# Gated mix of linear attention and squared-relu layer: hidden tiles fetched four and split two steps ahead, attention a step farther behind its numerators, the query-weight fold three products sooner

## The chip, the cores and the metric

The kernel runs on one core of one Trainium2 chip. The metric is the device time of one launch in microseconds, the median of several runs. The engines are TensorE (PE in the profile), VectorE (DVE), ScalarE (ACT), GpSimd (POOL) and SyncE (SP), whose queue issues nearly all DMA transfers here.

## The reference, cut to what matters

The output mixes two branches of the same input x (2048 rows, 512 columns) with one gate per row. Branch A is linear attention with 32 heads of 16 columns and a softmax feature map. Branch B is a dense layer with 1792 hidden units, whose activation is the square of relu.

```python
qkv = split_heads(x @ wqkv)                       # 32 heads of 16
pq = einsum("bhsd,hdf->bhsf", q, w_phi)           # the same for k
phi = concat([softmax(p), softmax(-p)])           # 32 features per head
kv, z = phi_k^T V, sum(phi_k)
o = (phi_q kv) / (phi_q z + 1e-6)
a = o @ wo
b = relu(x @ w1 + b1)**2 @ w2 + b2
g = sigmoid((x * gate_w).sum(-1))
return g * a + (1 - g) * b
```

## The kernel before, in words

**Products.** Everything is fp32. A product is made of three fp32r matmuls (`mm3`, L59 to 63): both factors are split into a high part (a copy on ACT, L56) and a low part (a subtraction on DVE or POOL, L57), and high·high (L61), high·low (L62) and low·high (L63) are added in one bank. L61 and L62 need only the first factor's high part; L63 needs its low part. Names ending in h and l are these parts.

**First stages, up to about 272 us of the span.** The product x·w1 is computed by a seven-product scheme (banks uX, uY, uZ) and merged with the keys and values (banks kX, kY, kZ). Relu and square give the hidden activations. They don't stay on the chip: each 128x512 tile is written to DRAM (`hkept`). Near the end comes `fold("q")` (L254): 128 small matmuls fold the feature map's weights `wphi` into the query weights, in four banks; four DVE transposes (L268) bring them to SBUF, and `wq_ready` splits them. The list `seq` holds the order of these products on PE, and `at(n, f)` hangs a call on a place in it.

**Last stage, the loop over t = 0 to 55.** A step t is one hidden tile: `down(t, c)` adds its product with a 128-row piece of w2 to four banks, in 12 matmuls of 128x512. I call these twelve d0, d1 and so on. Each tile is fetched from DRAM by `h_fetch` (tile `hin`), and `h_ready` splits it: `hh` on ACT, `hl` on POOL. There are four buffers for each of hh and hl (tags O0 and O1, two buffers each), and four for the ring "in", which hin shares with xnin, xin and wphi.

Branch A of one pair of 128-row pieces is a group p = 0 to 7, and `starts[p]` is its first step. The table `steps` says which of its parts come before which d:
- `do_q` of each of two pieces: 12 matmuls (I number these 16 projections q0 to q15), then on DVE the largest and smallest value of each head (L305, L306) and two subtractions (L307, L308), the exponential on ACT (L310), and sums and reciprocals on DVE (L315, L317).
- `do_q_scaled`: two products with z on POOL (`ez`, L508), a reduction and small operations on DVE (L510 to L517), the scaling (L321) and a transpose to `tb` (L525). After the second piece, tb is regrouped into `phiT` by four copies on ACT (L534) and twelve DMAs on SP (L536).
- `do_n`: 32 small matmuls give the numerators (`num`, L544; num0 to num7 by p), split to `oh` on ACT and `ol` on DVE.
- `attend` of each piece: 12 matmuls with the weights wo (att0 to att15), then a sum on DVE (L586) and, when both branches have met, the write of the row.

`gate_load` and `gate_dot` (tile xnin, L407) and `gates` (`ge`, L412) make the gates of the next 512 rows; `x_again` fetches the next x (xA... from `xkept`, or xin from the input, split to xS10 and xS11).

**What sets the order.** PE's order is the order of the code (`manual_schedule` for PE). DVE, ACT, POOL and the DMA queue are ordered by the scheduler, which follows the code's order, its own estimate of readiness, and priorities (`ahead`). On the chip every engine and every queue works in order: an instruction that waits holds up all behind it.

Of the kernel before, what the change touches and what calls it, by code (L numbers as in the profile page):

```python
# [21 lines left out]
NC = SB // P  # L22
# [13 lines left out]
def tile_gated_mix(ctx: ExitStack, tc: tile.TileContext, xT, xn, wqT, wkT, wphi, wv, wo, w1, b1, w2, b2, gw, out):  # L36
# [217 lines left out]
    def fold(nm):  # L254
        wph, t = st["wphi"], st["wT", nm]
        pss = [bank(f"fold{nm}") for r in range(4)]
        for g in range(NK):
            for q in range(4):
                for r in range(4):
                    rows, cols = slice(32 * r, 32 * r + 32), slice(g * P + 32 * r, g * P + 32 * r + 32)  # L260
                    nc.tensor.matmul(pss[r][32 * q:32 * q + 32, g * P:(g + 1) * P], wph[rows, cols],
                                     t[g][rows, :].rearrange("r (k q i) -> r k q i", q=4, i=32)[:, :, q, :],
                                     start=True, stop=True, skip_group_check=True)
        w = work.tile([P, 2, 4, NG, 32], F32, tag="phiT", name=f"w{nm}in", bufs=1).rearrange(
            "p u r g s -> p (u r g s)").rearrange("p (k g r s) -> p k g r s", k=NK, g=NK, r=4)
        for r in range(4):
            with ahead():
                nc.vector.transpose(w[:, :, :, r, :].rearrange("p k g s -> p g k s"),  # L268
                                    pss[r].rearrange("p (g k i) -> p g k i", g=NK, i=32))
        st["w", nm] = [w[:, k].rearrange("p g r s -> p (g r s)") for k in range(NK)]  # L270
# [219 lines left out]
    def h_fetch(t):  # L490
        i, f = divmod(t, NF)
        raw["h", t] = load(ring("hin"), hkept[ORDER_B[i], f])

    def h_ready(t):
        hi, lo = st["h", t] = [work.tile([P, 512], F32R, tag=f"O{t % 2}{j}", name="h" + j, bufs=2) for j in "hl"]
        split(raw["h", t], hi, lo, nc.gpsimd)
# [164 lines left out]
    seq, extra = [], {}  # L661
    at = lambda i, f, *a: extra.setdefault(i, []).append(lambda: f(*a))
# [105 lines left out]
    with tc.manual_schedule(engines={mybir.EngineType.PE}):  # L768
        warm_up()
        opening()  # L770

        us = u_stream([(0, g) for g in range(3, NPF)], (0, 2))
        vs = v_stream([(0, m, "kv") for m in range(NC)])
        seq = merged(us, vs)
        n0 = len(seq)
        PER = 15
        for g in range(3, NPF):
            b = PER * (g - 3)
            if g > 3:
                at(b - 8, w_sums, g, POOLE)  # L780
                at(b - 4, w_ready, g, 1)
            at(b + 1, w_ready, g, 2)
            at(b + 2, w_last, g, POOLE)
            at(b + 6, w_ready, g, 3)
            if g > 3:
                at(b + 1, w_save, g, 0)
            else:
                at(b + 1, w_save, g, 0)
            at(b + 3, w_save, g, 1)
            at(b + 5, w_save, g, 2)  # L790
            at(b + 9, w_save, g, 3)
            if g + 1 < NPF:
                at(b + 2, w_fetch, g + 1)
                at(b + 8, w_ready, g + 1, 0)
        at(24, x_fetch, 1)
        at(30, x_fetch2, 1)
        for kk in range(2):
            at(n0 - 14 + 2 * kk, x_sums, kk, ("S1", "S2"), POOLE)

        n1 = n0  # L800
        us1 = u_stream([(1, g) for g in range(NPF)])
        vs1 = v_stream([(1, m, "kv") for m in range(NC)], (0, NC - 1, "kv"))
        seq1 = merged(us1[:len(us1) - 5], vs1) + us1[len(us1) - 5:]
        seq += seq1
        for i, op in enumerate(XOPS):
            for kk in range(2):
                at(n0 + i - (4 if i < 3 else 1), x_ready, op, kk)
        for kk in range(2):
            at(n0, x_sums, kk, ("S3",), POOLE)
            at(n0 + 2, x_sums, kk, ("S4",), POOLE)  # L810
        per = len(seq1) / NPF

        def o1_raw():
            raw["w", 0, 0] = load(ring("w1in"), w1[0])

        at(n0 - 12, o1_raw)
        at(n0 - 6, w_ready, 0, 0)
        for g in range(NPF):
            b = n0 + int(per * g)
            if g:  # L820
                at(b - 9, w_again, g, 0)
            at(b - 7, w_again, g, 1)
            at(b - 3, w_again, g, 2)
            at(b + 2, w_again, g, 3)
        at(n0 + 4, lambda: nc.sync.dma_start(gwb, gw.partition_broadcast(P)))
        for c in range(NC):
            n = ORDER_B[0] * NC + c
            at(n0 + 10 + 3 * c, gate_load, n)
            at(n0 + 14 + 3 * c, gate_dot, n)
        at(n0 + 24, gates, ORDER_B[0])  # L830
        for i in range(0, NF, 4):
            fs = range(i, min(i + 4, NF))
            at(n0 + 9 + 3 * i, w2_prepare, fs)
            for k, f in enumerate(fs):
                at(n0 + 12 + 3 * i + 2 * k, w2_split, k, f)
        n2 = len(seq)

        def q_fetch():
            t = work.tile([P, 4 * D], F32, tag="tb", name="wqin", bufs=1)
            load_fold("q", wqT, [t[:, k * D:(k + 1) * D] for k in range(NK)])  # L840
            st["wphi"] = load(ring("wphi"), wphi)

        at(n2 - 20, q_fetch)
        seq.insert(n2 - 2, lambda: fold("q"))
        n2 += 1
        for f in range(4):
            at(n2 - 5 + f, w2_again, f)
        at(n2 - 1, h_fetch, 0)
        at(n2 - 1, h_fetch, 1)
        run()  # L850


        steps = {}
        when = lambda s, f, *a: steps.setdefault(s, []).append(lambda: f(*a))
        NT = NB * NF
        starts = (2, 7, 12, 18, 24, 30, 36, 42)
        for k in range(NK):
            when(0, wq_ready, k)
        x_again(0)
        when(1, kv_burst, (1, NC - 1, "kv"))  # L860
        when(3, kv_done)
        when(0, b2_load)
        for k in range(NK):
            when(4 + k, wo_fetch, k)
            when(6 + k, wo_ready, k)
        when(8, x_again, 1)
        when(starts[3] + 3, x_again, 2)
        when(starts[5] + 3, x_again, 3)
        for i in range(1, NB):
            b, s = ORDER_B[i], starts[2 * i] - 8  # L870
            for c in range(NC):
                when(s + c, gate_load, b * NC + c)
                when(s + 2 + c, gate_dot, b * NC + c)
            when(s + 6, gates, b)
        for p, s in enumerate(starts):
            for c in range(2):
                when(s + 2 * c, do_q, p, c)
                when(s + 2 * c + (3 if p == 0 else 1), do_q_scaled, p, c)
            when(s + 10, do_n, p)
            for c in range(2):  # L880
                when(s + 12 + c, attend, p, c)
        h_ready(0)
        for t in range(NT):
            for f in steps.get(t, ()):
                f()
            i, f = divmod(t, NF)
            if t + 2 < NT:
                h_fetch(t + 2)
            if t + 1 < NT:
                h_ready(t + 1)  # L890
            for g in (2 * t + 4, 2 * t + 5):
                if g < NF:
                    w2_again(g)
            if f == 0:
                st["d"] = [ubank(f"d{c}") for c in range(NC)]
            last = t == NT - 1
            now = () if t == NT - 2 else (t - 1, t) if last else (t,)
            for c in range(NC - 1 if last else NC):
                for u in now:
                    down(u, c)  # L900
            if last:
                ends = [bank(f"end{j}") for j in range(2)]
                sc = slice((NC - 1) * P, NC * P)
                for j, s in enumerate(halves):
                    for u in now:
                        mm3(ends[j][:, s], st["h", u], st["w2", u % NF], sc, s, u == now[0], u == t)
            if f < NF - 1:
                continue
            for c in range(NC):
                n = ORDER_B[i] * NC + c  # L910
                evict(n, st["d"][c], ALL)
                if last and c == NC - 1:
                    for e, d, s in zip((nc.sync, nc.scalar), ends, halves):
                        evict(n, d, s)
                        e.dma_start(out[n * P:(n + 1) * P, s], st["f", n][:, s])
                else:
                    out_done(n)
# [47 lines left out]
```

## Time and profile before

| | us |
|---|---|
| median of 3 runs | 558.26 |
| the three runs | 555.23, 558.42, 558.26 |
| the profiled execution's own time | 554.75 |
| its span in the trace | 553.0 |
| the loop's part of the span | from 272.7 (d0) to 549.4 |
| DMA moved | 108.92 MB, mean 197 GB/s |
| ACT busy in the span | 244.3, 44% |
| POOL busy in the span | 236.4, 43% |

The table is of one core, so there is no slower core to look for. A profile row of the timeline reads: start, duration, engine, line, operation, what is written <- what is read, shape, how many instructions in a row; in brackets the idle time just before and what ended it. SPq is the queue that issues DMAs; such a row's duration is the issue, not the transfer. A matmul of the loop has a duration of 0.39 us but overlaps with the next, so what counts is the distance between starts.

### The profile page before, as it was taken

Reading aid. Unit: us, or ns where it says so; the run is one execution under the profiler, and the core shown is the slowest. Engines: PE = TensorE matmul, PEld = TensorE weight load, DVE = VectorE, ACT = ScalarE, POOL = GpSimd, SP = SyncE. Lnnn points to the kernel's source line nnn. Section 1 sums busy time; section 2 is a strip of 40 time slices with the busy share of each in tenths; the row PEclk is TensorE's granted clock in tenths of the full one; section 3 lists DMA queues with packets and bytes.
Section 4 is the critical chain, followed back from the end, with each engine's and each line's share of the span. In section 5 each row is a group of like instructions: output and inputs, shape, how many; then the busy total and the mean of one; then the engine's idle time right before and its main releaser. Section 6 shows DMA issues by size and latency. Waiting matters only on the chain.

```text
span 553.0 us, 9651 instructions
## 1 busy us (share of the span) xinstructions
PE 505.1 (91%) x3532; PEld 396.2 (72%) x3532; DVE 425.7 (77%) x607; ACT 244.3 (44%) x399; POOL 236.4 (43%) x190
## 2 busy tenths in 40 slices
PE   7587679999998999999899699989999969999997
PEld 3355458877776888788688577767787848777776
DVE  4986759979999967766858989997879684787503
ACT  5485546446666565645543234242314323332320
POOL 3945743274235356320525434534345433434320
PEclk9799869999999999999999979989999998999999
DMA  8458487854368998999877363756235523135312
GB/s 299 176 210 307 153 286 261 292 197 162 115 211 293 317 347 295 336 353 335 299 257 239 95 192 104 234 152 200 84 122 156 146 79 95 39 83 166 82 35 76
DMA packets 66167, 108.92 MB, mean 197 GB/s; under 512 B 8264, under 2 KB 18248, under 8 KB 66120
## 3 DMA queue, kind: packets, MB, share of 16 engines
q1 hardware_dynamic: 65800, 107.91, 58.9%
q8 instruction: 28, 0.46, 0.4%
q10 hardware_dynamic: 288, 0.39, 0.2%
q14 instruction: 19, 0.16, 0.1%
q0 software_dynamic: 32, 0.01, 0.0%
HBM read 60.30 MB, written 41.68 MB: 184 GB/s over the span
## 4 chain that ended last, share of the span: by engine, by line
PE 45%; DVE 23%; DMA 11%; issue 7%; ACT 6%; SPq 5%; POOL 4%; DVEq 0%; POOLq 0%; ACTq 0%
PE d L61 5%; PE d L62 5%; PE d L63 5%; PE att L63 3%; SPq L536 2%; DMA w1in<-in_w 2%; DVE e L308 2%; PE att L62 2%; PE att L61 2%; PE uY L63 2%; PE uY L61 2%; DMA hin<-hkept 2%; DVE e L321 2%; PE uY L62 2%; DVE sm L315 2%
## 5 line engine op out<-in xcount | busy, mean ns | idle before, releaser
L57 POOL TENSOR_TENSOR hl<-hin,hh 128x512 fp32r<-128x512 f32 x56 | 73.7, 1325 | 130.9 <-ACT hh L56 128.1
L56 ACT ACTIVATE hh<-hin 128x512 fp32r<-128x512 f32 x56 | 34.7, 627 | 95.3 <-PE d L62 34.4
L221 POOL TENSOR_TENSOR t<-t,t 128x512 f32<-128x512 f32 x28 | 41.5, 1485 | 46.9 <-ACT t L220 34.3
L508 POOL TENSOR_TENSOR ez<-e,z 128x512 f32<-128x512 f32 x32 | 42.6, 1351 | 36.3 <-ACT e L310 31.0
L310 ACT ACTIVATE e<-e 128x1024 f32<-128x1024 f32 x32 | 33.8, 1058 | 47.3 <-DVE e L308 47.0
L315 DVE TENSOR_REDUCE sm<-e 128x64 f32<-128x1024 f32 x32 | 38.9, 1217 | 19.6 <-ACT e L310 19.5
L197 ACT ACTIVATE c<-c,b1c 128x512 f32<-128x512 f32 x42 | 29.9, 718 | 33.0 <-DVE c L212 33.0
L198 ACT ACTIVATE c<-c 128x512 f32<-128x512 f32 x56 | 34.8, 627 | 1.1
L534 ACT ACTIVATE phiT<-tb 32x512 f32<-32x512 f32 x32 | 20.1, 628 | 32.1 <-DVE tb L525 26.9
L480 POOL TENSOR_TENSOR w2in<-w2in,w2h 128x512 fp32r<-128x512 f32 x14 | 20.2, 1464 | 29.8 <-DMA w2in<-in_w 20.0
L510 DVE TENSOR_REDUCE dz<-ez 128x64 f32<-128x1024 f32 x16 | 19.5, 1218 | 17.2 <-POOL ez L508 17.2
L321 DVE TENSOR_TENSOR e<-e,w 128x1024 f32<-128x1024 f32 x16 | 21.6, 1350 | 0.3
L212 DVE TENSOR_TENSOR c<-uY,t 128x512 f32<-128x512 f32 x28 | 18.8, 676 | 3.9 <-PE uY L63 3.9
L321 DVE TENSOR_TENSOR e<-e,r 128x1024 f32<-128x1024 f32 x16 | 21.0, 1314 | 0.2
L525 DVE STREAM_TRANSPOSE tb<-e 128x1024 f32<-128x1024 f32 x16 | 19.7, 1238 | 0.3
L305 DVE TENSOR_REDUCE mx<-q 128x32 f32<-128x512 f32 x16 | 10.8, 675 | 9.0 <-PE q L63 9.0
L317 DVE RECIPROCAL r<-sm 128x64 f32<-128x64 f32 x32 | 17.4, 543 | 0.2
L57 DVE TENSOR_TENSOR ol<-num,oh 128x512 fp32r<-128x512 f32 x16 | 10.2, 677 | 9.1 <-ACT oh L56 9.1
L586 DVE SCALAR_TENSOR_TENSOR row<-b2b,rest,att 128x512 f32<-128x512 f32 x8 | 5.9, 739 | 14.6 <-PE att L63 14.6
L153 POOL TENSOR_TENSOR T23in<-w1in 128x256 f32<-128x256 f32 x6 | 6.1, 1009 | 23.0 <-DMA w1in<-in_w 23.0
L407 DVE SCALAR_TENSOR_TENSOR xnin<-xnin,gwb 128x512 f32<-128x512 f32 x16 | 14.0, 877 | 0.0
L61 PE MATMUL att<-woVt,oh 128*128 128x512 f32 x32 | 13.4, 419 | 0.0
(533 smaller groups left out, 1633.1 us busy)
## 6 DMA issues: line engine op xcount, KB each, us to landing
hkept<-c SPq DMA_DIRECT2D x56, 256.0 KB, 3.5
hin<-hkept SPq DMA_DIRECT2D x56, 256.0 KB, 2.9
phiT<-tb SPq DMA_DIRECT2D x96, 64.0 KB, 2.0
xin<-in_xT SPq DMA_DIRECT2D x20, 256.0 KB, 5.4
xnin<-in_xn SPq DMA_DIRECT2D x16, 256.0 KB, 2.8
out<-row SPq DMA_DIRECT2D x15, 256.0 KB, 2.2
w1in<-in_w SPq DMA_DIRECT2D x14, 256.0 KB, 3.7
w2in<-in_w SPq DMA_DIRECT2D x14, 256.0 KB, 4.2
```

Of the source, the lines that this page charges most:

```text
L56: nc.scalar.activation(hi, src, AF.Copy)
L57: elo.tensor_tensor(lo, src, hi.bitcast(F32), ALU.subtract)
L61: nc.tensor.matmul(o, ah[:, sa], bh[:, sb], start=first, stop=False, **kw)
L62: nc.tensor.matmul(o, ah[:, sa], bl[:, sb], start=False, stop=False, **kw)
L63: nc.tensor.matmul(o, al[:, sa], bh[:, sb], start=False, stop=last, **kw)
L197: nc.scalar.activation(t, src, AF.Relu, bias=b1c[:, f:f + 1])
L198: nc.scalar.activation(t, t, AF.Square)
L221: nc.gpsimd.tensor_tensor(t, t, st["t1", u], ALU.add)
L310: nc.scalar.activation(ef, ef, AF.Exp)
L315: nc.vector.tensor_reduce(sm, e3, AX.X, ALU.add)
L321: eng.tensor_tensor(e3, e3, w.unsqueeze(2).to_broadcast([P, 2 * H, DH]), ALU.mult)
L508: nc.gpsimd.tensor_tensor(ez[:, hs, :], e3[:, hs, :], zbc[half], ALU.mult)
```

## The change

The diff changes the schedule only; the arithmetic stays as it was.

```diff
-        seq.insert(n2 - 2, lambda: fold("q"))
+        seq.insert(n2 - 5, lambda: fold("q"))
...
-        at(n2 - 1, h_fetch, 0)
-        at(n2 - 1, h_fetch, 1)
+        for t in range(4):
+            at(n2 - 4 + t, h_fetch, t)
...
-        starts = (2, 7, 12, 18, 24, 30, 36, 42)
+        starts = (2, 7, 12, 18, 24, 30, 36, 41)
...
-                when(s + 2 + c, gate_dot, b * NC + c)
+                when(s + 1 + c, gate_dot, b * NC + c)
...
-                when(s + 12 + c, attend, p, c)
+                when(s + 13 + c, attend, p, c)
         h_ready(0)
+        h_ready(1)
         for t in range(NT):
...
+            if t + 4 < NT:
+                h_fetch(t + 4)
             if t + 2 < NT:
-                h_fetch(t + 2)
-            if t + 1 < NT:
-                h_ready(t + 1)
+                h_ready(t + 2)
```

In words: the fold stands three products sooner; hidden tiles are fetched four steps ahead instead of two, and split two steps ahead instead of one; each attend stands a step later; each gate dot a step sooner, and the last group starts at step 41 instead of 42.

On PE the attend of a group, put one step later, also changes places with the projections of later groups. In the words used above, the twelve-matmul items after three of the num read:

```
before  num1 d17 q6  d18 att2 d19 att3 q7  d20 d21 num2
after   num1 d17 q6  d18 d19  att2 q7  d20 att3 d21 num2
before  num3 d28 d29 att6 q10 d30 att7 d31 q11 d32 d33 num4 d34 d35 att8 q12 d36
after   num3 d28 d29 q10 d30 att6 d31 att7 q11 d32 d33 num4 d34 d35 q12 d36 att8
```

The other engines' orders come from the scheduler, so the built order is shown at three places.

First, POOL and the DMA queue ahead of num0. POOL's rows of before, where the two ez of a piece are POOL's part of q1, q2 and q3 in the last three pairs:

```order
L57 TENSOR_TENSOR hl<-hin,hh 128x512
L508 TENSOR_TENSOR ez<-e,z_3288 128x512
L508 TENSOR_TENSOR ez<-e,z_3290 128x512
L57 TENSOR_TENSOR hl<-hin,hh 128x512 x2
L508 TENSOR_TENSOR ez<-e,z_3288 128x512
L508 TENSOR_TENSOR ez<-e,z_3290 128x512
L57 TENSOR_TENSOR hl<-hin,hh 128x512 x3
L508 TENSOR_TENSOR ez<-e,z_3288 128x512
```

POOL's rows of the changed kernel, at the same pairs:

```order
L57 TENSOR_TENSOR hl<-hin,hh 128x512 x2
L508 TENSOR_TENSOR ez<-e,z_3296 128x512
L508 TENSOR_TENSOR ez<-e,z_3298 128x512
L57 TENSOR_TENSOR hl<-hin,hh 128x512 x2
L508 TENSOR_TENSOR ez<-e,z_3296 128x512
L508 TENSOR_TENSOR ez<-e,z_3298 128x512
L57 TENSOR_TENSOR hl<-hin,hh 128x512 x2
L508 TENSOR_TENSOR ez<-e,z_3296 128x512
```

Before, the group "x3" behind q2's ez is hl of steps 9, 10 and 11; now steps 9 and 10 stand ahead of q2's ez, and 11 and 12 behind it.

The DMA queue (SP) of before, from the fetches of steps 10 and 11 to the transfers of phiT for num0:

```order
L69 DMA hin<-hkept 128x512
L69 DMA xin<-in_xT 128x512 x2
L69 DMA hin<-hkept 128x512 x2
L428 DMA xA110h<-xkept 128x512
L428 DMA xA110l<-xkept 128x512
L428 DMA xA111h<-xkept 128x512
L536 DMA phiT<-tb 32x2x256 x12
L69 DMA hin<-hkept 128x512 x4
```

The same queue of the changed kernel, from the fetch of step 11:

```order
L69 DMA hin<-hkept 128x512
L69 DMA xin<-in_xT 128x512 x2
L69 DMA hin<-hkept 128x512
L428 DMA xA110h<-xkept 128x512
L536 DMA phiT<-tb 32x2x256 x12
L69 DMA hin<-hkept 128x512 x4
L428 DMA xA110l<-xkept 128x512
L69 DMA hin<-hkept 128x512 x2
```

Ahead of phiT stands now the fetch of step 12 instead of steps 10 and 11, and one xA instead of three. The fetch of step 12 takes a ring buffer that hl of step 11 frees, where that of step 11 took one from hl of step 9.

Second, ACT around the numerators of num1. Before:

```order
L310 ACTIVATE e<-e 128x1024
L56 ACTIVATE hh<-hin 128x512 x2
L412 ACTIVATE ge<-lg 128x4
L56 ACTIVATE oh<-num_3963 128x512
L56 ACTIVATE oh<-num_3964 128x512
L534 ACTIVATE phiT<-tb 32x2x256 x4
```

And in the changed kernel:

```order
L310 ACTIVATE e<-e 128x1024
L56 ACTIVATE hh<-hin 128x512 x2
L56 ACTIVATE oh<-num_3973 128x512
L56 ACTIVATE oh<-num_3974 128x512
L534 ACTIVATE phiT<-tb 32x2x256 x4
L56 ACTIVATE hh<-hin 128x512
L412 ACTIVATE ge<-lg 128x4
```

The gate's exponential (ge) stands now behind both oh and the copies of phiT.

Third, the DMA queue around phiT for num4, where the x of the last 512 rows (xin) is fetched. Before:

```order
L575 DMA out<-row 128x512 x2
L69 DMA hin<-hkept 128x512 x2
L69 DMA xin<-in_xT 128x512 x2
L69 DMA hin<-hkept 128x512
L536 DMA phiT<-tb 32x2x256 x12
L575 DMA out<-row 128x512
```

In the changed kernel:

```order
L69 DMA xnin<-in_xn 128x512
L69 DMA hin<-hkept 128x512 x2
L536 DMA phiT<-tb 32x2x256 x12
L575 DMA out<-row 128x512
L69 DMA xin<-in_xT 128x512 x2
L69 DMA hin<-hkept 128x512
```

The two xin stand now behind phiT's twelve transfers and behind a write of a row, which waits for the sum of att6 on DVE. On DVE their low parts (xS10l, xS11l) have moved from ahead of q10's features to ahead of q11's.

## The prediction

> **What bounds the kernel now.** I read the page first, then PE's waits, then PE's clock by stretches of the loop, and at each stretch that loses time the timelines of the engines around it. The page's busy time:
>
> ```profile
> PE 505.1 (91%) x3532; PEld 396.2 (72%) x3532; DVE 425.7 (77%) x607; ACT 244.3 (44%) x399; POOL 236.4 (43%) x190
> ```
>
> PE is the bound: it misses 48 us of 553.0, much of that in the first stages. What the change can win is what PE loses in the loop. PE's waits, with the total, the number of times and the longest (only the rows on d and att, which belong to the loop):
>
> ```profile
> PE att L63 <- DVE ol L57: 6.1, 5, 4.6
> PE d L63 <- POOL hl L57: 3.7, 1, 3.7
> PE d L61 <- DVE c L212: 2.3, 1, 2.3
> PE att L61 <- ACT oh L56: 1.3, 1, 1.3
> PE d L61 <- ACT hh L56: 0.6, 1, 0.6
> ```
>
> These are 14.0 us of idle time. To them comes what a slower clock costs behind the long ones. The windows view, by stretch:
>
> ```profile
> core 0: us, PE busy (x) PEld busy (x) DVE busy (x) ACT busy (x) POOL busy (x), PEclk, DMA share, GB/s
> 315.00:320.00 5.00, 2.16 (x5) 1.78 (x6) 5.00 (x6) 0.63 (x1) 4.02 (x3) 0.69 0.30 87
> 320.00:325.00 5.00, 5.00 (x15) 3.90 (x15) 3.69 (x6) 2.96 (x5) 1.28 (x1) 0.62 0.78 233
> 365.00:370.00 5.00, 3.42 (x11) 2.37 (x11) 4.97 (x12) 4.31 (x9) 0.00 (x0) 0.81 0.51 147
> 450.00:455.00 5.00, 0.42 (x1) 0.42 (x2) 4.36 (x8) 0.00 (x0) 2.91 (x3) 0.85 0.28 88
> 455.00:460.00 5.00, 5.00 (x13) 3.84 (x13) 3.25 (x4) 2.40 (x4) 0.00 (x0) 0.50 0.16 43
> ```
>
> PE is fully busy in 455 to 460 and yet does 13 matmuls: the granted clock is 0.50. So there are three losses: before 325 (d9), at 366 (att2) and at 450 to 460 (att8). PE's timeline at the first:
>
> ```profile
> 313.43 0.50 PE L61 MATMUL d<-w29h,hh 128*128 128x512 f32 x1 [0.57 <-ACT hh L56]
> ...
> 317.84 0.79 PE L63 MATMUL d<-w29h,hl 128*128 128x512 f32 x1 [3.68 <-POOL hl L57]
> 318.43 0.63 PE L61 MATMUL d<-w29h,hh 128*128 128x512 f32 x1
> ...
> 323.12 0.63 PE L63 MATMUL d<-w210h,hl 128*128 128x512 f32 x1
> ...
> 325.74 0.39 PE L61 MATMUL d<-w211h,hh 128*128 128x512 f32 x1
> ...
> 328.55 1.85 PE L544 MATMUL num<-phiT,kvb 64*32 64x256 f32 x32
> 330.33 0.50 PE L61 MATMUL q<-wq0h,xS10h 128*128 128x512 f32 x1
> ```
>
> From 318.43 to 323.12 lie 11 spaces of 0.426 us; d11, twelve matmuls from 325.74 to 328.55, takes at most 0.234 each. Thirteen slow matmuls cost 13 x 0.19 = 2.5 us. Idle time is 4.25 us, so the place costs 6.7.
>
> **The change part by part.** Hidden tiles sooner. The causes of the wait at d9, from the timelines of POOL, SP and DVE, and the page's row on the landing of phiT and xin:
>
> ```profile
> 313.00 3.56 POOL L508 TENSOR_TENSOR ez<-e,z 128x512 f32<-128x512 f32 x2 [6.97 <-ACT e L310]
> 316.52 2.50 POOL L57 TENSOR_TENSOR hl<-hin,hh 128x512 fp32r<-128x512 f32 x2
> ...
> 313.26 4.88 SPq L69 DMA_DIRECT2D hin<-hkept  x2
> 319.62 8.14 SPq L536 DMA_DIRECT2D phiT<-tb  x12
> ...
> 316.49 1.23 DVE L525 STREAM_TRANSPOSE tb<-e 128x1024 f32<-128x1024 f32 x1
> ...
> phiT<-tb SPq DMA_DIRECT2D x96, 64.0 KB, 2.0
> xin<-in_xT SPq DMA_DIRECT2D x20, 256.0 KB, 5.4
> ```
>
> hl of step 9 stood on POOL behind the ez of q2, which waited until 313.00. In the new order it stands ahead of them, so d9 no longer waits, and PE reaches num0 6.7 us sooner. But num0 needs phiT, and phiT is not sooner by as much. tb is ready at 316.49 + 1.23 = 317.7. SP now meets the fetch of step 12, whose buffer hl of step 11 frees; that hl is the first behind ez on POOL, done at about 316.52 + 1.25 = 317.8. Two issues of 0.4 us later, at 318.7, phiT starts: 0.9 us before 319.62. The end of num0 is set by phiT in both kernels (8.14 us of issues and 2.0 of landing give 329.8, and q4 starts at 330.33). So PE now stands from about 321 to 327.6, and the 6.7 us is not won but moved. Behind a wait that long I expect the slow clock as in the rows above. My value: 2.5 - 0.9 = +1.6 us. Lower end: phiT starts at tb's end and nothing is slowed, -1.9; upper end: slow clock and 1 us of later issue, +3.5. I take +1.6, since the wait is nearest to the 3.68 and 4.61 us that did slow PE.
>
> [...]
>
> The other fetches and splits are at no cost: in the loop's later steps no row of PE's waits names hl or hh. SP issues as many transfers as before. The gate dot one step sooner moves 0.7 us of DVE work within a stretch where DVE does all the waiting work in order anyway: nothing.
>
> Attend a step later, at att2. ACT's and PE's timelines:
>
> ```profile
> 365.63 0.20 ACT L412 ACTIVATE ge<-lg 128x4 f32<-128x4 f32 x1 [4.68 <-DVE xnin L407]
> 365.74 1.07 ACT L56 ACTIVATE oh<-num 128x512 fp32r<-128x512 f32 x2
> ...
> 366.37 0.50 PE L61 MATMUL att<-woXS40h,oh 128*128 128x512 f32 x1 [1.30 <-ACT oh L56]
> ...
> 367.38 0.50 PE L63 MATMUL att<-woXS40h,ol 128*128 128x512 f32 x1 [0.28 <-DVE ol L57]
> ```
>
> oh stood behind ge, which waited for the gate dots on a late DVE. Now oh stands ahead of ge, and att2 comes one d (2.7 us) later. Both alone cover 1.58 us. Gone are 1.58 us of idle and some eight slow matmuls (1.5), with 0.3 for restarting: -3.4. Ends: -3.4 and 0.
>
> At att8, from the timelines of PE, DVE and SP:
>
> ```profile
> 442.77 1.09 PE L544 MATMUL num<-phiT,kvb 64*32 64x256 f32 x32
> 454.58 0.80 PE L63 MATMUL att<-woXS40h,ol 128*128 128x512 f32 x1 [4.61 <-DVE ol L57]
> ...
> 430.30 0.69 DVE L57 TENSOR_TENSOR xS11l<-xin,xS11h 128x512 fp32r<-128x512 f32 x1 [2.06 <-ACT xS11h L56]
> 444.26 0.65 DVE L305 TENSOR_REDUCE mx<-q 128x32 f32<-128x512 f32 x1
> 453.84 1.28 DVE L57 TENSOR_TENSOR ol<-num,oh 128x512 fp32r<-128x512 f32 x2
> ...
> 427.07 7.62 SPq L536 DMA_DIRECT2D phiT<-tb  x12
> ```
>
> ol stands on DVE behind q11's chain: from its features at 444.26 to ol 9.6 us. That chain was late since q10's features waited for xS11l. Now att8 stands behind q12 and d36, so 2 x 2.7 = 5.4 us later than today's 449.97, at 455.4. PE as a whole comes about 2.1 us sooner by the terms above and att4's, so ol is wanted at 453.3. Is it there? xin is now issued behind phiT and a write: 427.07 + 7.62 + 0.5 = 435.2, lands 5.4 later at 440.6, two copies on ACT and two subtractions on DVE end at about 443.2, then q11's chain, 9.6: ol at 452.8. That is 0.5 us of margin if DVE and SP come no sooner than today. They do: q10 is projected one item sooner and doesn't wait for xin, and phiT, with it xin, follows a DVE that has lost 2.06 us of waiting and the lateness from 366; that adds up to 3 us. So the wait goes, 4.61 us of idle and 13 slow matmuls (2.5): -7.2 with 0.1 of restart. Ends: -7.2 and 0.
>
> Three other att waits, what is left of the first row (6.1 - 4.6 - 0.3 = 1.2 us), are 0.4 to 0.5 us each, and 2.7 us more lead covers them: -1.2. Ends: -2.6, with restarts and all, and 0. After them nothing is late next but DVE's own chain; PE goes on with d.
>
> The fold, from DVE's timeline:
>
> ```profile
> 264.06 0.69 DVE L364 TENSOR_TENSOR k<-kY,t 128x512 f32<-128x512 f32 x1 [2.03 <-PE kY L63]
> 272.24 1.22 DVE L321 TENSOR_TENSOR e<-e,r 128x1024 f32<-128x1024 f32 x1
> 273.38 2.50 DVE L268 STREAM_TRANSPOSE wqin<-foldq 128x512 f32<-128x512 f32 x4
> ```
>
> Its four banks include kY's, which L364 frees at 264.75, just where the fold now stands on PE: a wait of some 0.8 us. The four transposes come ahead of L321 and of the uY evictions (L212) on DVE. The 2.3 us that d0 waited for such an eviction goes over to the last product, and the kvps matmuls that need L321's result come no sooner. Best end: the 2.3 goes and 0.8 comes, -1.5. Worst end: kvps comes later by the 2.50 us of transposes, +2.5. I take 0, between them.
>
> Sum: 0 + 1.6 - 3.4 - 7.2 - 1.2 = -10.2 us. Against the profiled execution's 554.75 this is 544.6; that execution is 3.5 us under the median of 558.26, from which it would be 548.1. Runs lie at both places, so I subtract from the middle, 556.5: 546.3 us.
>
> **The rivals.** One: att8 still waits. For it: the margin of 0.5 us, and two more issues ahead of xin, of which the write waits for att6's sum on DVE. Against it: the lead that q10 gains. Price: 7.2 back, 553.5.
>
> Two: the time before num1 governs all. DVE was busy throughout 315 to 320 and 4.97 of 5.00 in 365 to 370; if the slack moves but DVE is still late, att2 and att8 both wait: 546.3 + 10.6 = 556.9, no change. Against it: at 450 to 455 DVE too has idle time, so that lateness is one of order.
>
> Three, slower: phiT late at every num, as at num0. Place: the fetches four steps ahead stand on SP before phiT, wait for hl on POOL, and hl for ez. At num4 today phiT is complete at 427.07 + 7.62 + 2.0 = 436.7, 6.1 us before 442.77. If the queue holds phiT up by 10 us at three of the num, each waits 4 us and loses 2.5 to the clock: 19.5, thus 565.8. It decides from a delay of about 9 us on. For it: num0 shows it; against it: the 6.1.
>
> Four, better: num0 costs nothing or less, and the restarts go too. From 554.75: -1.9 - 3.4 - 7.2 - 2.6 = 539.7.
>
> That the deeper fetch does nothing, as hh and hl have four buffers already, would leave the wait at d9 and take away num0's: 544.7, within the forecast.
>
> **How the numbers follow.** Forecast 0.62 (541 to 550 by itself), rival one 0.14, two 0.08, three 0.06, four 0.10. A measurement of this kernel can tell about 1% from no change, 5.6 us: faster means below 552.7. Faster: 0.62 + 0.10 and 0.06 of rival one, where part of att8's wait is won, 0.78; within 1%: 0.08 of one and 0.08 of two, 0.16; slower: 0.06. The range 539 to 554 leaves out two and three and little more.
>
> **What would show it.** In the changed profile PE's waits should have no d behind hl, and no att behind oh or a long ol; num0 should wait 6 to 7 us for phiT, with a granted clock near 0.5 behind it; att2 and att8 should run into d without a gap. Wrong would be: an att8 still idle for ol (then xin's place is to be looked at), a num other than num0 that waits for phiT, a fold that waits longer than 1 us with kvps late.

## The result, and the profile after

The changed kernel is slower by about 0.9%, which is under the 1% that the prediction called no change: 560.1 us against 555.65 us, medians of 20 runs each, ratio 1.0087 with a 95% interval of 1.0064 to 1.0110. The forecast was 546.3 us and the range 539 to 554. The profiled execution of the changed kernel took 560.03 us.

The page of the changed kernel, its span and busy times:

```profile
span 558.2 us, 9654 instructions
PE 506.3 (91%) x3532; PEld 398.8 (71%) x3532; DVE 423.1 (76%) x607; ACT 244.3 (44%) x399; POOL 239.9 (43%) x190
```

The engines do the same work. Not all of the 5.2 us between the two spans belongs to the change. The timelines of TensorE give the last matmul of the last kY product, up to which TensorE's order is the same, and the last matmul of all; in the changed kernel:

```profile
267.65 0.39 PE L63 MATMUL kY<-KT41h,A221l 128*128 128x512 f32 x1
...
554.48 0.28 PE L63 MATMUL end<-w213h,hl 128*128 128x256 f32 x1
```

and in the kernel before:

```profile
263.63 0.39 PE L63 MATMUL kY<-KT41h,A221l 128*128 128x512 f32 x1
...
549.15 0.28 PE L63 MATMUL end<-w213h,hl 128*128 128x256 f32 x1
```

From there to the end are 285.5 us before and 286.8 after. Second profiles of both (below) gave 284.4 and 289.4, and start times of 266.6 and 265.7. So the first stages vary by 2 to 3 us from run to run, and what follows the last kY, the fold included, lost 1 to 5 us. Nothing of the 10.2 us forecast is left in the time. TensorE's waits in the changed kernel, the rows from the fold on:

```profile
PE d L61 <- DVE row L598: 6.1, 2, 4.2
...
PE uY L61 <- DMA O3h<-wkept: 4.4, 1, 4.4
...
PE num L544 <- DVE ge L415: 3.4, 1, 3.4
...
PE num L544 <- DMA phiT<-tb: 1.9, 1, 1.9
```

No att waits any more, and no d waits for hl: 14.0 us of the old waits are gone. In their place stand 15.8 us in these four rows: a hidden-layer product for its weights O3h, num0 twice, and two d that wait for evictions (L598). An eviction is the DVE operation that reads a finished bank, so that the next products may use it. The profile puts num0's longer wait down to the gates' ge because that ended just then; num0 doesn't read ge. It reads phiT, whose twelve issues run from 326.57 to 334.36 in this kernel, so both of its waits are taken for phiT. The windows view shows the slow clock behind them (columns as in the prediction: the clock is the third number from the right):

```profile
280.00:285.00 5.00, 4.29 (x10) 3.46 (x11) 1.36 (x3) 2.84 (x6) 0.00 (x0) 0.50 0.93 298
335.00:340.00 5.00, 3.94 (x35) 2.41 (x36) 4.93 (x11) 2.44 (x5) 1.76 (x2) 0.50 0.88 261
420.00:425.00 5.00, 3.91 (x12) 3.18 (x13) 4.84 (x7) 2.61 (x5) 3.48 (x3) 0.76 0.43 156
490.00:495.00 5.00, 2.72 (x7) 2.17 (x8) 5.00 (x8) 3.25 (x5) 2.58 (x3) 0.59 0.39 95
```

In three of the four, DVE is busy for 4.84 to 5.00 of 5 us. The stretches between the ends of the num tell where time went, in us from one end to the next:

| stretch | before | after |
|---|---|---|
| last kY to the kvps matmuls | 14.5 | 19.9 |
| to the end of num0 | 52.3 | 50.5 |
| num0 to num1 | 26.3 | 27.0 |
| num1 to num2 (att2) | 29.5 | 25.7 |
| num2 to num3 | 29.1 | 28.5 |
| num3 to num4 (d28) | 28.6 | 32.0 |
| num4 to num5 (att8) | 36.0 | 28.5 |
| num5 to num6 (d42) | 29.2 | 35.5 |

(The table is read off the timelines of the two kernels; behind num6 the items differ.) The first row runs from start to start, the second from the start of the kvps matmuls. The forecast gains at att2 and att8 came, 3.8 and 7.5 us; they were paid back at the fold (5.4), at d28 (3.4) and at d42 (6.3).

The fold, timelines of TensorE and of the DMA queue in the changed kernel:

```profile
275.95 0.39 PE L63 MATMUL uZ<-S41h,O1l 128*128 128x512 f32 x1
280.70 0.76 PE L61 MATMUL uY<-A220h,O3h 128*128 128x512 f32 x1 [4.36 <-DMA O3h<-wkept]
...
273.21 0.99 SPq L69 DMA_DIRECT2D hin<-hkept  x1
274.25 0.42 SPq L488 DMA_DIRECT2D w28l<-w2kept  x1
275.51 0.32 SPq L181 DMA_DIRECT2D O3h<-wkept  x1
```

O3h has one buffer. An earlier uY product frees it, and it is reloaded for the last uY. Before, the fold (1.9 us) and three products stood between the two; now only the products do. The fold, moved ahead of both, covers nothing of the reload, and on the DMA queue the reload stands behind a hidden tile and w2 tiles and goes out at 275.51.

At d42, timelines of DVE and TensorE:

```profile
489.03 0.65 DVE L305 TENSOR_REDUCE mx<-q 128x32 f32<-128x512 f32 x1
...
490.81 0.67 DVE L308 TENSOR_TENSOR e<-mn,q 128x512 f32<-128x512 f32 x1
491.40 1.39 DVE L598 SCALAR_TENSOR_TENSOR row<-d,rest,row 128x512 f32<-128x512 f32 x2
...
492.28 0.77 PE L61 MATMUL d<-w20h,hh 128*128 128x512 f32 x1 [4.23 <-DVE row L598]
```

A block of 14 steps ends with d41; d42 needs its bank empty. Here q14 stands ahead of d41 (start 41 and not 42), so q14's features stand ahead of the eviction on DVE, and nothing stands between d41 and d42 on TensorE. Before, att10 and q14 stood between them.

### The profile page after: what moved, and what is told of

Its sections match the earlier page's. It is cut to its first block, busy times and chain, and to the rows that moved or that the text cites. A ratio compares the mean times of both kernels' runs of the same rounds, so it can differ in the third digit from the quotient of the medians.

```text
span 558.2 us, 9654 instructions
## 1 busy us (share of the span) xinstructions
PE 506.3 (91%) x3532; PEld 398.8 (71%) x3532; DVE 423.1 (76%) x607; ACT 244.3 (44%) x399; POOL 239.9 (43%) x190
## 4 chain that ended last, share of the span: by engine, by line
PE 52%; DVE 22%; DMA 10%; issue 6%; POOL 4%; ACT 3%; SPq 3%; DVEq 0%; POOLq 0%; ACTq 0%
PE d L61 7%; PE d L62 7%; PE d L63 7%; PE att L61 2%; PE att L62 2%; PE att L63 2%; DMA hin<-hkept 2%; DMA w1in<-in_w 2%; DVE e L308 2%; PE uY L63 2%; PE uY L61 2%; PE q L61 2%; PE uY L62 2%; PE q L62 2%; PE q L63 2%
## 5 line engine op out<-in xcount | busy, mean ns | idle before, releaser
L57 POOL TENSOR_TENSOR hl<-hin,hh 128x512 fp32r<-128x512 f32 x56 | 76.4, 1369 | 143.9 <-ACT hh L56 132.8
L221 POOL TENSOR_TENSOR t<-t,t 128x512 f32<-128x512 f32 x28 | 43.7, 1564 | 44.7 <-ACT t L220 32.1
L508 POOL TENSOR_TENSOR ez<-e,z 128x512 f32<-128x512 f32 x32 | 42.0, 1334 | 23.9 <-ACT e L310 23.7
L480 POOL TENSOR_TENSOR w2in<-w2in,w2h 128x512 fp32r<-128x512 f32 x14 | 19.6, 1423 | 32.2 <-DMA w2in<-in_w 20.4
L510 DVE TENSOR_REDUCE dz<-ez 128x64 f32<-128x1024 f32 x16 | 19.4, 1215 | 16.6 <-POOL ez L508 16.6
L525 DVE STREAM_TRANSPOSE tb<-e 128x1024 f32<-128x1024 f32 x16 | 19.9, 1241 | 0.3
L544 PE MATMUL num<-phiT,kvb 64*32 64x256 f32 x256 | 10.2, 411 | 5.4 <-DVE ge L415 3.4
L61 PE MATMUL d<-w20h,hh 128*128 128x512 f32 x16 | 8.4, 525 | 6.1 <-DVE row L598 6.1
```

The lines of the kernel that those rows point to most:

```text
L57: elo.tensor_tensor(lo, src, hi.bitcast(F32), ALU.subtract)
L61: nc.tensor.matmul(o, ah[:, sa], bh[:, sb], start=first, stop=False, **kw)
L221: nc.gpsimd.tensor_tensor(t, t, st["t1", u], ALU.add)
L508: nc.gpsimd.tensor_tensor(ez[:, hs, :], e3[:, hs, :], zbc[half], ALU.mult)
```

## The experiments

All ratios are to the kernel before, run on the same chip. Theory A said that the losses are places, each to be undone by itself. Theory C said that DVE is the bound in the loop, so that a wait taken away comes back where TensorE next needs DVE. The other letters are explained in the expectations.

**The fold back.** Edit of the changed kernel:

```diff
-        seq.insert(n2 - 5, lambda: fold("q"))
+        seq.insert(n2 - 2, lambda: fold("q"))
```

> The changed kernel with the fold back two products before the end. Theory A (the fold used to cover the reload of the w1 tile O3h, whose single buffer the product uY39 frees): the 4.4 us wait of the last uY for O3h and the slow clock behind it go, d0's 2.3 us wait for an eviction comes back, last kY to kvps takes about 14.5 us as before instead of 19.9, and the time falls by about 5 us from the changed kernel's, to a ratio to before of about 0.998. Rival B (the reload is late because four hidden-tile fetches now stand ahead of it in the DMA queue): the wait for O3h stays at 3 us or more, ratio about 1.009 as for the whole change. In both the 4.2 us wait of d42 for the eviction stays.

Measured: 554.38 us, ratio 1.0003 (0.9968 to 1.0038), 0.8% under the whole change. The last uY waits 0.4 us and no longer for O3h; last kY to kvps takes 12.9 us, less than in the kernel before, as d0's wait is gone too. Theory A holds for this place; by rival B of the expectation the wait would have stayed. The edit also changes the order of the DMA queue, so by itself it doesn't part the two causes; the fold alone, below, is for that.

**The start back.** Edit of the changed kernel (with a start of 42 the last attends would fall behind the last step, so they stay):

```diff
-        starts = (2, 7, 12, 18, 24, 30, 36, 41)
+        starts = (2, 7, 12, 18, 24, 30, 36, 42)
...
-                when(s + 13 + c, attend, p, c)
+                when(min(s + 13, NT - 2) + c, attend, p, c)
```

> The changed kernel with the last group's start back at 42 (its two attends stay at steps 54 and 55). Theory A (with start 41 the projection q14 stands one step ahead, its features go ahead of the eviction of the four banks on DVE, and d42 has to wait): the eviction stands ahead of q14's features again, d42's wait of 4.2 us and the slow clock behind it go, num5 to num6 takes about 29 us instead of 35.5, ratio to before about 0.997. Rival C (DVE is the bound there and att10 merely waits instead): num5 to num6 stays above 33 us, with a wait of an att for ol, ratio about 1.008.

Measured: 555.9 us, ratio 1.0041 (1.0006 to 1.0076). That is 0.5% under the whole change, where theory A expected 1.2%. The stretch from num5 to num6 takes 32.2 us, between the 29 of A and the 33 of C, and no att waits for ol, which C had expected. The eviction stands ahead of q14's features now, and still TensorE waits, from its timeline:

```profile
492.69 0.47 PE L61 MATMUL d<-w20h,hh 128*128 128x512 f32 x1 [1.84 <-DVE row L598]
```

**The fold alone**, moved in the kernel before:

```diff
-        seq.insert(n2 - 2, lambda: fold("q"))
+        seq.insert(n2 - 5, lambda: fold("q"))
```

> The kernel before with only the fold moved three products sooner. Theory A: the last uY waits 3 to 5 us for O3h here too, last kY to kvps takes 18 to 20 us, the time rises by about 5 us, ratio about 1.009. Rival B (fetches in the queue): no such wait, since only two tiles are fetched early, ratio 0.997 to 1.002.

Measured: 555.83 us, ratio 1.0039 (1.0004 to 1.0073), and 17.2 us from the last kY to kvps. A loss of half the size, and the wait has another name (TensorE's timeline):

```profile
280.95 0.50 PE L61 MATMUL uY<-A220h,O3h 128*128 128x512 f32 x1 [2.59 <-DVE c L212]
```

That is an eviction behind the fold's four transposes on DVE, about the prediction's upper end of 2.5 us. So the rest of the 5 us needs the deeper fetch as well: neither A nor B alone. The 0.4% needn't all be the fold's: in this profile d11 waits 7.5 us for hh and 0.7 for hl, where before d9 waited 4.3; why was not tested.

**Fold and start back**, both edits above:

> The changed kernel with the fold back and the last start back at 42: what is left is the deeper fetch and split of hidden tiles, the earlier gate dot and the later attend. Theory A: both losses go and the gains at att2, att8 and the small att waits (12 us in the changed kernel's trace) stay: about 548 us against 555.65, ratio about 0.987; d28's wait of 1.9 us for an eviction and num0's wait for phiT stay. Rival C (DVE bound, waits only move): ratio 0.997 or more.

Measured: 552.55 us, ratio 0.9954 (0.9917 to 0.9991). Both losses go, yet only 0.5% is gained of the 1.3% that theory A expected. d28 and d42 wait 3.5 and 3.7 us for evictions. The ratio lies between A's 0.987 and C's 0.997 or more, nearer to C, and the interval reaches into C's range only.

**The attend alone** in the kernel before, with the same guard for the last group:

```diff
-                when(s + 12 + c, attend, p, c)
+                when(min(s + 13, NT - 2) + c, attend, p, c)
```

> The kernel before with only the attend a step later (the last group's two stay at steps 54 and 55). Theory C: the att waits (att2, att8 and the small ones, 8 us with the slow clock 12) go and come back in part at d28 and d42 as waits for evictions of 2 to 4 us each with a slow clock behind; d9's wait for hl stays: ratio 0.992 to 1.000. Theory A would give the full gain, 0.98.

Measured: 553.21 us, ratio 0.9995 (0.9963 to 1.0026). TensorE has no att wait left, and waits at d14, at d42 and, for 2.3 us, at num0 in their place:

```profile
349.03 0.50 PE L61 MATMUL d<-w20h,hh 128*128 128x512 f32 x1 [1.95 <-DVE row L601]
...
489.23 0.66 PE L61 MATMUL d<-w20h,hh 128*128 128x512 f32 x1 [4.90 <-DVE row L598]
```

The att terms, 11.8 us and the largest part of the forecast, are worth nothing by themselves: at most 2 us by the interval.

**The hidden tiles alone**: the kernel before with the lines of h_fetch and h_ready of the change.

> The kernel before with only the hidden tiles fetched four and split two steps ahead. d9's wait for hl goes and a wait for phiT at num0 of about the same length takes its place, att2's and att8's waits stay: ratio 0.997 to 1.003. If the deeper fetch delays phiT or the late x on the DMA queue, ratio above 1.004.

Measured: 552.57 us, ratio 0.9987 (0.9965 to 1.0009). As expected, d9's wait is gone, and num0 waits 3.60 and 2.97 us. att2's wait went too; att4 waits 2.6 us and att8 3.1 for ol.

**The gate dots left out**, on the kernel with fold and start back; the gates of the last three blocks are made from the first block's sums:

```diff
-                when(s + 1 + c, gate_dot, b * NC + c)
```

> The kernel with fold and last start back (0.9954 of before), and with the twelve gate dots of the last three blocks of 512 rows left out (their gates are made from the first block's sums). That takes 12 operations of 0.65 to 1.6 us, about 10 us, off DVE alone. Theory C (the chain on DVE from one projection's features to the next, 14.4 us on average, is as long as what TensorE has to do between them, so a wait taken away at an att comes back where TensorE next needs DVE): the waits of d28 (3.5 us) and d42 (3.7 us) for evictions shrink by 2 us or more each or go, num0 starts 1 to 3 us sooner, ratio to before 0.975 to 0.985. Theory A (those waits come from the place of the evictions behind q9's features and q13's chain, not from DVE's load): the two waits stay within 1 us, ratio 0.992 to 0.996.

Measured: 540.35 us, ratio 0.972 (0.9675 to 0.9765). 12 us go with 12 operations on DVE, and no product less on TensorE. With the dots goes more: the gates' small operations stand ahead of the loop, and the xnin tiles are no longer read. The waits at num0 and d28 are gone and d42 waits 1.8 us; d14 now waits 2.5. Theory C's range, somewhat past its end. Most of it comes early: q6's features start at 360.0 instead of 369.9, and from there to q15's it takes 130.1 us instead of 133.6.

**num0 later**, on the kernel with fold and start back:

```diff
-            when(s + 10, do_n, p)
+            when(s + (12 if p == 0 else 10), do_n, p)
...
-                when(min(s + 13, NT - 2) + c, attend, p, c)
+                when((s + 15 if p == 0 else min(s + 13, NT - 2)) + c, attend, p, c)
```

> The same kernel with num0 two steps later (and its two attends two steps later), so that q4, d12 and d13 stand ahead of it while phiT is on its way. Theory A: the 6 us of idle time at num0 and the slow clock behind it go, 7 to 8 us less, ratio about 0.983. Theory C: the waits at num0 go, but TensorE is only further ahead of DVE, so d28 or an earlier place waits longer by most of it; ratio 0.990 to 0.996.

Measured: 550.82 us, ratio 0.9916 (0.9879 to 0.9954). Of some 7 us at num0, 2 are kept; d13 now waits for hh, num1 for phiT and d42 for its eviction, while d28's wait is gone. Theory C's range.

**Second profiles of both kernels.**

> The kernel before, for a second profile: whether the last kY product, at 263.6 us in the first profile and at 265.8 to 269.7 in five of other kernels with the same code up to about 230 us, is as early again. If the first stages vary from run to run, it lies anywhere in 263 to 270; the loop from there takes 285.8 us within 1.

> The changed kernel, for a second profile: the last kY anywhere in 263 to 270 if the first stages vary, the rest 287.1 us within 1.5, with the same waits (uY for O3h, num0, d28, d42). A rival: these waits vary by more than 1 us from run to run, and the first profile was a lucky one for the rest, 3 us short of the 4.5 us by which the medians differ.

Measured: 556.56 and 560.57 us. The last matmul of the last kY started at 266.58 and 265.68, so the first stages vary. After_again's waits at d28 and d42 were 3.48 and 5.87 us against 1.88 and 4.23 in the first profile: the rival holds, the new waits vary by over 1 us.

**The dots on POOL and ACT**, on the kernel with fold and start back; for the later blocks:

```diff
+            nc.gpsimd.tensor_tensor(t, t, gwb, ALU.mult)
+            nc.scalar.activation(t, t, AF.Copy, accum_out=st["lg"][:, n % NC:n % NC + 1])
```

> The kernel with fold and last start back (0.9954 of before), with the twelve later gate dots done by POOL (a product) and ACT (a copy that sums), so that DVE loses the same 10 us as where they were left out (0.972), but the result is whole. Theory C: most of that gain comes, ratio 0.973 to 0.983; what is lost against 0.972 is what the twelve products of about 1.3 us each on POOL delay ez and hl. A rival: POOL, which has ez in the same chain, takes its place, and the ratio stays at 0.99 or more.

> The same with num0 two steps later. Theory C: with DVE relieved TensorE can use the 6 us that it waited at num0, so this is faster than the kernel without the later num0 by 2 to 5 us, ratio 0.967 to 0.977. If DVE is still the bound, the two are equal within 0.4%.

Measured: 558.47 us, ratio 1.0090 (1.0061 to 1.0119), and with the later num0 562.62 us, 1.0163 (1.0119 to 1.0206). Theory C's ranges missed in both; in the first the rival that the expectation names, POOL in DVE's place, came out. The stretch from 270 to 556 us shows POOL busy for 129.2 us where it was 112.0, and DVE for 205.1 where it was 211.4. POOL's ez is in the same chain as DVE's work, and DVE waits 23.2 us for ez where it waited 19.4. That loading POOL costs more than DVE gains fits this.

**Dummy reductions where the dots were**, over a constant tile:

```diff
-                when(s + 1 + c, gate_dot, b * NC + c)
+                when(s + 1 + c, dummy)
```

> The kernel without the twelve later gate dots (0.972; their gates come from the first block's sums), with a maximum over a constant 128x512 tile on DVE in the place of each: twelve operations of 0.68 us, which hold no buffer of the ring, wait for no transfer and hold up no gate. Theory C (DVE's time in the chain is what counts): most of the gain goes again, ratio 0.986 to 0.996, with waits for evictions at d28 or d42 of 3 us or more. Theory D (not DVE's time, but that the dots held ring buffers that the next hidden tiles or xin wanted, and made in-order DVE wait for their transfers): the gain stays, ratio 0.970 to 0.978.

Measured: 541.53 us, ratio 0.9746 (0.9719 to 0.9772). By the expectation's wording this is theory D. But the dummies are cheaper than what they stand for. The groups by line, of the kernel with fold and start back (280 to 550 us):

```profile
L407 DVE SCALAR_TENSOR_TENSOR xnin<-xnin,gwb 128x512 f32<-128x512 f32 x12 | 10.7, 890 | 0.5 <-DMA xnin<-in_xn 0.5
L414 DVE TENSOR_SCALAR inv<-ge 128x4 f32<-128x4 f32 x3 | 1.5, 509 | 1.6 <-ACT ge L412 1.6
L417 DVE TENSOR_SCALAR eps<-inv 128x4 f32<-128x4 f32 x3 | 1.4, 463 | 0.0
L407 DVE DVE_READ_ACCUMULATOR xnin<-xnin,gwb 128x1 f32 x12 | 1.0, 80 | 0.0
```

and of the kernel with the dummies:

```profile
L412 DVE TENSOR_REDUCE mx<-gwb 128x32 f32<-128x512 f32 x12 | 7.8, 672 | 0.0
```

So 7.8 us came back for some 15 that went (the gates' small operations went from the loop too), and DVE was less busy by 11.6 us in all. Even so, 7.8 us of work on DVE cost 1.4 us of time against the kernel without dots (0.9746 to 0.972; by the two intervals at most some 4 us), which is not one for one. DVE waits 5.6 us for TensorE's projections in this kernel's loop and 1.6 in the one without dots, so it has some time to spare there.

**The dots kept, their sums not used** (the gates of all blocks come from the first block's sums and stand ahead of the loop): the twelve later dots write to another small tile.

> The kernel with fold and last start back (0.9954 of before); the twelve later gate dots stay on DVE with their buffers and their times, but their sums are not used (the gates of all blocks are made from the first block's sums, and so stand ahead of the loop). Without the dots this gave 0.972, with dummy reductions in their place 0.9746. Theory E (what costs is the round trip dot, exponential on ACT, four small operations on DVE, which stands on in-order DVE ahead of q6's features, 4.2 us in the trace of the parent, and likewise for the other blocks): most of the gain comes, ratio 0.974 to 0.984. Theory D (ring buffers held by the dots until DVE is there, so late hidden tiles and x): ratio 0.990 to 0.996.

Measured: 547.93 us, ratio 0.9883 (0.9847 to 0.9919), between the two ranges. The windows view from 270 to 556 us, for the kernel with fold and start back, then this one, the dummies, and no dots (DVE is the third busy time):

```profile
270.00:556.00 286.00, 265.23 (x1595) 211.61 (x1594) 211.39 (x324) 90.73 (x144) 111.98 (x86) 0.97 0.46 140
```

```profile
270.00:556.00 286.00, 263.41 (x1595) 210.46 (x1593) 204.80 (x311) 90.52 (x141) 113.29 (x86) 0.97 0.46 140
```

```profile
270.00:556.00 286.00, 259.44 (x1592) 207.99 (x1590) 199.75 (x299) 90.44 (x140) 112.99 (x86) 0.99 0.45 139
```

```profile
270.00:556.00 286.00, 259.98 (x1593) 208.58 (x1591) 197.00 (x287) 90.92 (x141) 111.80 (x86) 0.99 0.45 138
```

DVE's busy time falls by 6.6, 11.6 and 14.4 us; the time falls, by the ratios times 555 us, by 3.9, 11.5 and 13.0. TensorE has the same products to do in all four. So less work on DVE goes with less time, but the work isn't shown to be the whole price: the unused dots, 10.7 us on DVE, cost 9 us against the kernel without them, and the dummies' 7.8 us only 1.4. What else the dots cost (their transfers, the ring buffers that they hold, their places) stays open.

**Low parts of x on POOL**, on the kernel with the later num0:

```diff
-            split(src, *t)
+            split(src, *t, nc.gpsimd)
```

> The kernel with fold and last start back and num0 two steps later (0.9916 of before), with the low parts of the x tiles that come from the input (xS10l, xS11l of two blocks) split on POOL instead of DVE: four operations of 0.65 to 1.6 us off DVE, four of about 1.3 us onto POOL, where twelve dots cost 7 us net. Theory C: DVE gains 3 to 4 us just ahead of q4's and q11's features, ratio 0.983 to 0.990. The rival that POOL is as tight: 0.991 or more.

Measured: 545.83 us, ratio 0.9848 (0.9813 to 0.9884), with nothing left out and faster than both kernels. It lies in theory C's range. Four operations moved to POOL help where twelve hurt.

**The gates earlier** on top of that:

```diff
-            b, s = ORDER_B[i], starts[2 * i] - 8
+            b, s = ORDER_B[i], starts[2 * i] - 11
```

> The fastest whole kernel so far (fold and last start back, num0 two steps later, x lows on POOL: 0.9848) with the gate loads, dots and gates of the later blocks three steps sooner. Theory E: the exponential's round trip is off DVE's way to q6's and q10's features, since DVE has other work between; 2 to 5 us, ratio 0.975 to 0.981. Theory D: the ring is held as long, only sooner, ratio 0.983 to 0.99.

Measured: 556.02 us, ratio 1.0027 (1.0000 to 1.0054), so both theories' ranges missed: d0 waits 5.1 us for an eviction on DVE and d28 4.5 us. Work put earlier on DVE seems to have stood ahead of what TensorE needed; it wasn't traced further.

## Why the prediction was wrong

**The step that failed** is the sentence behind the three att terms: "After them nothing is late next but DVE's own chain; PE goes on with d." DVE's own chain was the bound there, and d isn't free of it: at steps 14, 28 and 42 the d need their banks emptied by DVE. So the three att terms, -11.8 us in the sum, were worth 0.3 us, with at most 2 by the interval (attend alone, 0.9995). Two more steps failed beside it: the fold, put at 0, and the last start, put at nothing without a reason (below). DVE's waits in the loop of the changed kernel (290 to 520 us) show the chain:

```profile
DVE dz L510 <- POOL ez L508: 16.6, 11, 3.2
DVE sm L315 <- ACT e L310: 10.6, 8, 2.4
DVE mx L305 <- PE q L63: 5.2, 1, 5.2
DVE inv L414 <- ACT ge L412: 1.0, 1, 1.0
DVE row L586 <- PE att L63: 0.7, 1, 0.7
```

DVE waits for TensorE's projections once, at q0, and never again; beyond that it waits 0.7 us for an att and 0.5 for kvt, and nearly all else is POOL and ACT within its own chain. From q6's features to q15's the changed kernel takes 373.7 to 503.9, 130.2 us for nine projections. In these DVE is busy for 103.2 and waits 23.9 for POOL's ez and ACT's exponential. TensorE has 25 d, 9 projections and 9 att of 2.72 us and 4 num of 1.1 to do between the same two projections: 121.4 us. So TensorE can't gain on DVE there. In the kernel before it wasn't so all along: DVE waited for q8 and q12, for q12 2.6 us, right behind the late att8. The att waits were where TensorE met DVE; without them it met DVE at the evictions.

The attend alone shows this (0.9995); the kernels with less work on DVE fit it. The outcome has the reason of rival two, "if the slack moves but DVE is still late", with a chance of 0.08, but not its place: that rival has att2 and att8 wait, and they didn't. The rival's counter-argument, that DVE idles at 450 to 455, took a wait for POOL's ez inside the chain (1.46 us) for spare time.

Point by point:
- *d9 and num0 (+1.6).* Right in its mechanism: the wait at d9 went, num0 waited 1.94 + 3.43 us, the clock behind it was 0.50, phiT started at 326.57, right behind the fetch of step 12 and one xA. The size was off: the hidden tiles alone gave 0.9987, at most 0.5 us more by the interval. phiT came 2.3 us sooner there, counted from the last kY (53.7 us behind it, 56.0 before), and not 0.9.
- *att2 (-3.4), att8 (-7.2), small ones (-1.2).* The waits went as worked out; as gains they were not kept.
- *The fold (0, at worst +2.5).* Wrong in the changed kernel: +5.4 us from the last kY to kvps in the first profiles, +3.8 in the second, and 0.8% of the time. The wait for kY's bank was 0.4 us. The working listed banks and DVE, and missed that the fold had covered the reload of O3h. Alone, without the deeper fetch, it cost 0.4%, 2.2 us, within the range given.
- *The last start at 41.* Not costed at all: it costs 0.5%, by q14's features ahead of the eviction and by nothing standing between d41 and d42.
- *The gate dot (0).* Not tried alone. The dots as such aren't free: without them the kernel was 2.3% faster.

The parts add up, within their intervals of some 0.3%: attend alone -0.05%, hidden tiles alone -0.13%, fold 0.4% alone and 0.8% taken out of the whole, start 0.5% taken out of the whole, against 0.87% for the whole.

**Open.** How much of the 12 us of the dots is their work and how much the ring buffers that they hold was not told apart. Dots kept but unused gave 3.9 us of it, with DVE's busy time falling by 6.6; the dummies cost less for each microsecond on DVE than the dots. And why d28 waited 1.9 us in one profile and 3.5 in the other stays open.

## What to carry to other kernels

A wait that ends on a chain of another engine is won only as far as that chain has slack: before adding it up, compare the time that the chain takes for a stretch (here 130.2 us for nine projections) with what the waiting engine has to do in it (121.4), and see whether the chain's engine ever waits for it. If it doesn't, look for the next place where the two meet. Here work taken off the chain was worth most (2.3% without the dots), and a rearrangement little (0.05% for the attend, 0.4% for the later num0). Ask of every moved instruction also what it used to cover: a reload into a single buffer, or the emptying of a bank.

## What the runs showed of the hardware that was not expected

Here the length of a wait didn't alone decide whether the clock fell. 1.88 us at d28 in the changed kernel were followed by a granted clock of 0.76 in 420 to 425; in the kernel before, 2.28 us at d0 were followed by none lower than full (1.00 in 275 to 290). Right ahead of the wait at d28 stand the 32 small matmuls of num3; whether they have a part in it is not shown here.

In one place a small operation on DVE took as long as a large one on POOL beside it. In the kernel with fold and start back, from the timelines of DVE and POOL:

```profile
367.42 1.27 DVE L414 TENSOR_SCALAR inv<-ge 128x4 f32<-128x4 f32 x1 [1.64 <-ACT ge L412]
...
367.37 2.54 POOL L57 TENSOR_TENSOR hl<-hin,hh 128x512 fp32r<-128x512 f32 x2 [7.58 <-DMA phiT<-tb]
```

Four elements per partition take 1.27 us there, half of POOL's two hl, and 0.10 us in the changed kernel at 334.62, where POOL does nothing from 333.9 to 338.2. The small operation ends at 368.69, as the first hl does by half of the 2.54 (368.64). What held it that long is not shown by these rows.
